# Where the first decay table of a chunked recurrence is kept: PSUM or SBUF

## The chip, the cores and the metric

The kernel runs on one core of a Trainium2 chip. The metric is the device time of one launch in microseconds (us). Engines are named as in the profile: PE is TensorE (matmul), DVE is VectorE, ACT is ScalarE, POOL is GpSimd, and SP issues most of the transfers. The runs lie between 174.58 and 174.9 us.

## The reference

Two parts, one after the other. The first is a linear recurrence over 768 steps, for 4 sequences, 8 heads and head size 48; the second is a two-layer network over the 3072 resulting rows with a smooth gate between.

```python
def _attn_ref(r, k, v, w, u):                 # r, k, v: (4, 8, 768, 48); w, u: (8, 48)
    ...
    for t in range(S):
        kt, vt, rt = (k[:, :, t].copy(), v[:, :, t].copy(), r[:, :, t].copy())
        cur = np.einsum('bhd,bhe->bhde', u[None] * kt, vt)
        y[:, :, t] = np.einsum('bhd,bhde->bhe', rt, state + cur)
        state = w[None, :, :, None] * state + np.einsum('bhd,bhe->bhde', kt, vt)

def _moe_ref(x, w_in, w_out):                 # (3072, 384) x (384, 2048), then x (2048, 384)
    h = x @ w_in
    g = np.where(h >= 1, h, np.where(h <= -1, 0.0, (h + 1) ** 2 / 4))
    return (g @ w_out).astype(np.float32)
```

## The kernel before

**The work and its names.** The 768 steps are cut into 6 chunks of 128 rows, one row per partition. A *group* g is one chunk of two sequences: groups 0 and 1 are the first chunk of sequences 0, 1 and of 2, 3, groups 2 and 3 the second chunk, and so on to 11. A *unit* is one sequence of a group; `Ks.0.1` is step `Ks` of group 0, unit 1, and `T.2` is step `T` of unit number 2, that is group 1, unit 0. Groups 0 and 1 are handled by unit, in tiles of 128x384 (8 heads of 48); later groups as a whole, 128x768.

**The decay.** Inside a chunk, decay is put on the operands: row t of R is multiplied by w^(t-64), row t of K by w^(63-t). The two tables of these powers are made on ACT by `exp(scale * log w)`, with a scale per partition (`dn_col` for K, `up_col` for R) and log w spread over all partitions by a matmul (`bcw`, tile `wb` in PSUM). The kernel makes each of them twice: at the start in PSUM, as the two halves of tile `tab` (steps `Wdn_p`, `Wup_p`, line 264), and a little later in SBUF, as `Wdn` and `Wup` (lines 257, 253). Groups 0 and 1 read `tab`, later groups read `Wdn` and `Wup`.

**The steps of a unit.** `load.K`, `load.R`, `loadV` are transfers from SP's queue. `Ks` and `Rs` (line 334) are the decayed K and R in bf16. `KU` (line 344) is K times u, `RKU` (351) R times that, `usum` (364 on DVE, 362 on ACT) its sum over a head, `V` the cast of V, `V2` (376) V times that sum (the profile shows its tile as `V`). `T` and `TT` turn `Ks` and `Rs` on PE and copy them out of PSUM; `A` (413) is the product of the turned two; `AT` masks it, either on DVE (428) or as a copy on ACT (419) and a select on POOL (423). `Sp` (439) and `Y` (448, 453) are the matmuls with V and with the state, `Tm` (483; 491 in the first chunk) and `decay` (496, POOL) the step of the state, `sbf` its bf16 copy, `y` (475) the output rows, `X` and `xT` their turn. Then `mm1` (533, tile `hp`), `relu` (541), `square` (546), `gate` (551, tile `gt`) and `mm2` (561, tile `op`) are the network.

**What sets the order.** A string `ORDER` lists every step; one token is a step with its numbers, `@D`, `@P` or `@A` for the engine and `:` with buffer numbers. Each engine does its instructions in the order of this list, and waits by semaphores only for what it reads or overwrites. The loads of the weights (`w_in`, `w_out`) stand on POOL's queue, between POOL's products: the first two pieces of `w_in` behind `Rs.2.0`. `~n` on a token puts n small matmuls on zeros ahead of a step on PE.

**Where the tiles lie.** PSUM has two tiles of one bank (`bank0`, `bank1`) and three tiles of two banks (`h0` to `h2`), shared by tag. `tab` lies in `h2` until the last product of group 1 has read it. POOL's instructions here read and write SBUF only.

Of the kernel before, what the change touches and what calls it, by code (L numbers as in the profile page):

```python
# [39 lines left out]
loadV.1.1 RKU.1.1@P AT.0.0 load.R.2.0:1 Ks.1.1@D V.1.1@A T.1:0~2 Tm.1@D usum.0.1@A Y.0:1~16 AT.2.0:0 TT.1@D:0 y.0:1  # L40
T.3:1~7 warm.6.h.2 V2.0.1@D Sp.0:0~4 usum.1.0@A:0 TT.3@A:1 A.1:2 X.0:1~4 Tm.0@D load.K.2.0:1 Sp.3:0 xT.0@A:1
Ks.2.0@D:0 A.3:0 Y.2:1~4 AT.1.1:1 Rs.2.0@P:0 Tm.3@D loadV.2.0:0 w_in.0 w_in.1 V2.1.0@P:0 T.5:1~8 sbf.1@A T.4:2~2
TT.5@A:1 AT.1.0 w_out.0 y.2:1 AT.3.0:2 w_in.2 Y.1:0~4 warm.2.h.0 A.5:1 y.1:2 usum.1.1@D X.1:1~2 Y.3:0~4 AT.5.0:0
TT.4@A:2 V2.1.1@P mm1.0.0.0:2 xT.1@A A.4:0~7 y.3:0 AT.4.0:2 X.2:1~4 load.K.3.0:2 V.2.0@A:1 xT.2@A:0 X.3:0 KU.2.0@P:1
mm1.0.0.1 mm1.0.1.0:0 w_out.2 xT.3@A mm1.0.1.1 RKU.2.0@D:0 usum.2.0@D:1 w_out.1 Sp.5:1 V2.2.0@P:1 mm1.1.1.-1:1
relu.0.0:1 Tm.5@D:1 Y.5:1~2 load.R.3.0:1 square.0.0:1 relu.0.1:0 gate.0.0:0 sbf.0@D square.0.1:0 Y.4:0~2 y.5:1 y.4:2
mm1.1.0.-1:2 gate.0.1:8 relu.1.1:1 X.4:0~2 xT.4@D:2 square.1.1:1 relu.1.0:0 gate.1.1:9 mm2.0.0.0:1 mm1.0.2.-1:0 Sp.4:0
Tm.4@D:0 mm1.0.3.-1:1 square.1.0:0 decay.5 mm2.0.1.0:0 gate.1.0:4 relu.0.2:0 square.0.2:1 Ks.3.0@P:2 KU.3.0@D:1
mm1.1.2.-1:2 gate.0.2:3 mm2.0.0.1 relu.0.3:1 sbf.2@D mm2.0.0.2 square.0.3:0 gate.0.3:0 w_out.3 mm1.1.3.-1:0 Rs.3.0@D:2
load.K.4.0:0 loadV.3.0:0 KRT.K.3:0 mm2.0.0.3 KRT.R.3:1 mm2.0.1.1 relu.1.2:0 square.1.2:1 mm2.0.1.2 relu.1.3:1  # L50
RKU.3.0@P:0 gate.1.2:8 o.0.0@A:1 X.5:1 usum.3.0@D:1 xT.5@A mm2.0.1.3 square.1.3:1 mm1.2.3.-1:2 o.0.1@A mm2.1.0.0:1
sbf.3@A V.3.0@D:1 Sp.6:0 gate.1.3:6 mm2.1.0.1 decay.4 mm2.1.0.2 A.7:1 relu.2.3:0 mm2.1.0.3 A.6:0 load.R.4.0:0
Ks.4.0@P:1 Tm.6@D:0 V2.3.0@P:1 o.1.0@A:0 AT.7.0:3 Sp.7:0 Y.7:1 AT.6.0:1 loadV.5.0:1 mm1.2.0.-1:1 Tm.7@D:1 load.K.5.0:1
decay.6 Y.6:0 mm1.2.2.-1:0 square.2.3:1 y.6:1 relu.2.0:1 y.7 load.R.5.0:2 square.2.0:0 Rs.4.0@P:1 gate.2.3:0
relu.2.2:0 mm2.1.1.0:1 mm2.1.1.1 xT.6:0 KRT.R.4:1 KRT.K.4:0 square.2.2:1 V.5.0@A:4 gate.2.0:9 gate.2.2:3 mm2.1.1.2
mm1.2.1.-1:2 relu.2.1:1 sbf.4@A loadV.4.0:1 square.2.1:1 decay.7 mm2.2.0.0:0 mm2.1.1.3 o.1.1@D KU.5.0@P:0 mm1.3.1.-1:1
relu.3.1:1 gate.2.1:6 mm1.3.2.-1:0 RKU.5.0@P:0 mm2.2.1.0:1 KU.4.0@D:0 mm2.2.0.1 sbf.5@D square.3.1:0 usum.5.0@D:0
gate.3.1:5 Rs.5.0@P:0 RKU.4.0@P:1 mm1.3.0.-1:2 mm2.2.1.1 load.K.6.0:2 relu.3.2:0 mm2.2.0.2 square.3.2:1 out.0
mm2.2.0.3 Ks.5.0@P:2 out.1 A.8:1 gate.3.2:4 A.9:0 mm2.2.1.2 usum.4.0@D:1 V.4.0@A:1 V2.4.0@P:1 relu.3.0:1 KU.6.0@P:1
# [44 lines left out]
def kernel(  # L104
# [157 lines left out]
    def table(what, i, col):  # L262
        t = tiles["tab"][:, i, :DM].rearrange("p (h d) -> p h d", h=H)
        nc.scalar.activation(flat(t), flat(tiles["wb"]), AF.Exp, scale=col, bias=0.0)
# [64 lines left out]
    def scaled(e, bk, g, j, what):  # L329
        j0, j1 = span(g, j)  # L330
        if j == 0:
            tiles[what + "s", g] = padded[what + "s"][bk[0]]
# [1 line left out]
        engines[e].tensor_mul(of_unit(dst, j0, j1)[:, :, :, :D], rep(tab, j1 - j0), of_unit(tiles[what, g], j0, j1))  # L334
# [322 lines left out]
```

## Time and profile before

| | us |
|---|---|
| median of 3 runs | 174.81 (174.58 to 174.9) |
| the profiled execution | 174.86 |
| its span (first to last instruction) | 173.1 |
| busy: PE, DVE, ACT, POOL | 164.1, 137.5, 133.5, 111.3 |

In the profile's rows an instruction is named by engine, line and out<-in, with the number of the tile left out; in brackets stands the idle time of the engine just before it, and what ended that. `PEld` is PE's load of weights. In the chain that ended last, each row is a stretch of work that released the next one; "issue" is time in which the engine waited for nothing that the profile shows. A timeline row that ends in x2 holds two instructions and the time of both. PE's matmuls overlap, so that a row's time is longer than its distance to the next. Rows of the windows view give, for each stretch, its length and for each engine busy time and count, and at the end the granted clock of PE (1.00 throughout), the share of the DMA engines and GB/s.

### The profile page before, as it was taken

What the parts mean: (1) busy time and instruction counts of PE and PEld (TensorE: products, weight loads), DVE (VectorE), ACT (ScalarE), POOL (GpSimd) and SP (SyncE); (2) the same over time, 40 slices, a digit from 0 to 9 for tenths busy, and PEclk for the clock granted to TensorE, in tenths of its full rate; (3) what the DMA queues carried; (4) which work ended last, traced back from release to release, by engine and by line L of the source; (5) the groups of instructions that cost most, each with busy time, mean ns of one, the idle gap of its engine ahead of it and who ended that gap; (6) DMA issues with size and microseconds to landing.
All of it is one profiled execution on the core that took longest, in us unless ns stands there. A gap on an engine that the chain in (4) does not pass through costs nothing.

```text
span 173.1 us, 4227 instructions
## 1 busy us (share of the span) xinstructions
PE 164.1 (95%) x1712; PEld 125.7 (73%) x1712; DVE 137.5 (79%) x175; ACT 133.5 (77%) x193; POOL 111.3 (64%) x92
## 2 busy tenths in 40 slices
...
GB/s 115 210 208 232 204 191 200 182 204 213 205 167 188 202 253 201 125 196 246 153 204 205 202 223 175 229 121 207 162 253 127 139 0 140 0 45 140 0 91 91
...
## 3 DMA queue, kind: packets, MB, share of 16 engines
...
q10 hardware_dynamic: 148, 0.13, 0.2%
q14 instruction: 6, 0.05, 0.1%
...
## 4 chain that ended last, share of the span: by engine, by line
PE 73%; DVE 9%; DMA 6%; SPq 4%; issue 3%; POOL 2%; ACT 1%; ACTq 0%
PE op L561 34%; PE hp L533 31%; DMA w_in_sb<-in_moe_w_in_dram 4%; SPq L311 4%; DVE gt L551 3%; PE A L413 3%; DMA R<-in_r_dram 2%; PE Y L448 2%; PE Y L453 2%; DVE Rs L334 1%; PE Sp L439 1%; POOL Rs L334 1%; DVE Tm L483 1%; DVE AT L428 1%; ACT sq L546 1%
## 5 line engine op out<-in xcount | busy, mean ns | idle before, releaser
L533 PE MATMUL hp<-xT,w_in_sb 128*128 128x256 bf16 (+1 forms) x600 | 70.1, 268 | 0.6 <-DVE AT L428 0.4
L561 PE MATMUL op<-w_out_sb,gt 128*128 128x384 bf16 (+2 forms) x400 | 69.6, 320 | 0.0
L551 DVE SCALAR_TENSOR_TENSOR gt<-sq,hp 128x1024 bf16<-128x1024 f32 x48 | 57.8, 1215 | 8.9 <-ACT sq L546 8.4
L533 PEld LDWEIGHTS <-w_in_sb 128*128 128x128 bf16 x600 | 55.4, 98 | 9.6 <-DVE gt L551 0.7
L541 ACT ACTIVATE pt<-hp 128x1024 f32<-128x1024 f32 x48 | 48.7, 1017 | 10.3 <-PE hp L533 9.7
L546 ACT ACTIVATE sq<-pt 128x1024 f32<-128x1024 f32 x48 | 50.5, 1058 | 2.9 <-DVE gt L551 2.0
L561 PEld LDWEIGHTS <-gt 128*128 128x128 bf16 x400 | 36.8, 98 | 20.4 <-DVE gt L551 0.5
L428 DVE TENSOR_TENSOR AT<-A,umask 128x1024 bf16<-128x1024 f32 x22 | 26.5, 1219 | 4.1 <-PE A L413 4.1
L351 POOL TENSOR_TENSOR RKU<-R,KU 128x768 f32<-128x768 f32 (+1 forms) x13 | 20.4, 1572 | 10.2 <-DMA R<-in_r_dram 6.3
L344 POOL TENSOR_TENSOR KU<-K,u_bc 128x768 f32<-128x768 f32 (+1 forms) x11 | 17.6, 1600 | 5.2 <-DMA K<-in_k_dram 5.2
L496 POOL TENSOR_TENSOR state<-Tm,wCm 128x384 f32<-128x384 f32 x16 | 16.8, 1053 | 1.6 <-DVE Tm L483 0.8
L334 POOL TENSOR_TENSOR Rs<-Wup,R 128x768 bf16<-128x768 f32 x9 | 16.4, 1826 | 2.1 <-DMA R<-in_r_dram 2.1
L334 POOL TENSOR_TENSOR Ks<-Wdn,K 128x768 bf16<-128x768 f32 x9 | 16.4, 1824 | 1.5 <-PE Sp L439 1.5
L376 POOL TENSOR_TENSOR V<-V,diag 128x768 f32<-128x768 bf16 (+1 forms) x11 | 15.3, 1390 | 2.8 <-DVE diag L364 2.4
L212 ACT COPY oo<-op 128x384 f32<-128x384 f32 x18 | 8.5, 473 | 10.7 <-PE op L561 9.2
L475 DVE TENSOR_TENSOR yy<-Y,V 128x384 bf16<-128x384 f32 x18 | 9.7, 553 | 3.8 <-PE Y L453 3.0
L453 PE MATMUL Y<-V,AT 128*128 128x48 bf16 x192 | 11.0, 183 | 0.3 <-POOL AT L423 0.3
L483 DVE TENSOR_TENSOR Tm<-Sp,state 128x384 f32<-128x384 f32 x16 | 8.8, 552 | 2.9 <-PE Sp L439 2.5
L364 DVE TENSOR_REDUCE diag<-RKU 128x16 f32<-128x768 f32 (+1 forms) x12 | 10.5, 879 | 0.0
L453 PEld LDWEIGHTS <-AT 128*128 128x128 bf16 x192 | 9.4, 96 | 1.5 <-issue 0.5
L216 ACT CAST V<-VF 128x768 bf16<-128x768 f32 (+1 forms) x11 | 8.1, 739 | 0.7 <-DMA VF<-in_v_dram 0.7
L448 PE MATMUL Y<-state_bf,RT 128*128 128x96 bf16 x72 | 8.5, 204 | 0.0
...
## 6 DMA issues: line engine op xcount, KB each, us to landing
...
```

Of the source, the lines that this page charges most:

```text
L334: engines[e].tensor_mul(of_unit(dst, j0, j1)[:, :, :, :D], rep(tab, j1 - j0), of_unit(tiles[what, g], j0, j1))
L344: engines[e].tensor_mul(of_unit(tiles["KU", g], j0, j1), of_unit(tiles["K", g], j0, j1), rep(u_bc, j1 - j0))
L351: engines[e].tensor_mul(of_unit(tiles["RKU", g], j0, j1), of_unit(tiles["R", g], j0, j1), of_unit(tiles["KU", g], j0, j1))
L376: engines[e].tensor_mul(tiles["V2", g][:, hs, :], tiles["V", g][:, hs, :], tiles["diag", g][:, hs].unsqueeze(2).to_broadcast([P, hs.stop - ...
L428: nc.vector.tensor_mul(t.rearrange("p i n t -> p (i n) t"), tiles.pop(("A", n)).rearrange("p i n t -> p (i n) t"), umask.unsqueeze(1).to_b ...
L453: nc.tensor.matmul(t[:, 2 * p + i, :], tiles["AT", n][:, i, p, :], tiles["V", g][:, j * H + 2 * p + i, :], start=(c == 0), stop=True, skip ...
L496: nc.gpsimd.tensor_mul(states[(g % BP) * UNITS + j], tiles.pop(("Tm", n)), wCm)
L533: nc.tensor.matmul(hp[:, f, cols], w_in_sb[:, i, n0 : n0 + P], tiles["xT", g][:, units, i, :], start=(i == 0), stop=(i == nK - 1), skip_gr ...
L541: nc.scalar.activation(tiles["pt", g, q], tiles["hp", g, q], AF.Relu, bias=0.5, scale=0.5)
L546: nc.scalar.activation(tiles["sq", g, q], tiles.pop(("pt", g, q)), AF.Square, bias=0.0)
L551: nc.vector.scalar_tensor_tensor(out=gt, in0=tiles.pop(("sq", g, q)), scalar=1.0, in1=tiles.pop(("hp", g, q)), op0=ALU.min, op1=ALU.max)
L561: nc.tensor.matmul(t, tiles["gt", g, q][:, f, j * P : (j + 1) * P], w_out_sb[:, n, cols], start=(n == 0), stop=(n == nF - 1),)
```

## The change

The table for K is no longer made in PSUM first. Step `Wdn_p` goes; step `Wdn`, which writes to SBUF, moves to its place, and the one of later is gone with it. `tab` now holds one table, that for R, in one bank instead of two, and is taken from PSUM by `Wup_p`. `Ks` reads `Wdn` in all groups; `Rs` of groups 0 and 1 still reads `tab`. Besides these, `ORDER` is the same, token for token.

```diff
-... u_bc@A Wdn_p:2 load.K.0.0:2 Wup_p wcol:1 wCm Ks.0.0@D:1 V.1.0@A:0
+... u_bc@A Wdn load.K.0.0:2 Wup_p:2 wcol:1 wCm Ks.0.0@D:1 V.1.0@A:0
...
-loadV.0.0:1 V.0.0@D:2 Wdn loadV.0.1 V.0.1@A usum.0.0@D:1 KU.0.1@P RKU.1.0@P:1 Wup load.R.0.1 Ks.0.1@D RKU.0.1@P
+loadV.0.0:1 V.0.0@D:2 loadV.0.1 V.0.1@A usum.0.0@D:1 KU.0.1@P RKU.1.0@P:1 Wup load.R.0.1 Ks.0.1@D RKU.0.1@P Rs.0.1@D
...
-    def table(what, i, col):
-        t = tiles["tab"][:, i, :DM].rearrange("p (h d) -> p h d", h=H)
-        nc.scalar.activation(flat(t), flat(tiles["wb"]), AF.Exp, scale=col, bias=0.0)
-        tiles["tab", what] = t
-
-    @step
-    def Wdn_p(e, bk):
-        tiles["tab"] = psum(f"h{bk[0]}", [P, 2, 4 * P], F32, "tab")
-        table("K", 0, dn_col)
-
     @step
     def Wup_p(e, bk):
-        table("R", 1, up_col)
+        t = psum(f"h{bk[0]}", [P, 4 * P], F32, "tab")
+        tiles["tab"] = t[:, :DM].rearrange("p (h d) -> p h d", h=H)
+        nc.scalar.activation(flat(tiles["tab"]), flat(tiles["wb"]), AF.Exp, scale=up_col, bias=0.0)
...
-        dst, tab = tiles[what + "s", g], tiles["tab", what] if g < TABLES else {"R": Wup, "K": Wdn}[what]
+        dst, tab = tiles[what + "s", g], tiles["tab"] if what == "R" and g < TABLES else {"R": Wup, "K": Wdn}[what]
```

Two places show it in the engines' own order. On ACT, at the start, with the semaphores waited for in brackets; before:

```order
L212 COPY u_bc<-ub 128x384 [waits PE_49]
L264 ACTIVATE tab<-wb,dn_col 128x384 [waits DVE_49,PE_49]
L264 ACTIVATE tab<-wb,up_col 128x384 [waits Activation_49]
L287 ACTIVATE wc_col<-wc 128x4 [waits PE_49]
L290 COPY wCm<-wc_col 48x4x48 [waits DVE_49,Activation_49]
L290 COPY wCm<-wc_col 48x4x48
L216 CAST V<-VF 128x384 [waits DMAHW4_49]
L212 COPY TT<-T 128x1024 [waits PE_49]
L257 ACTIVATE Wdn<-wb,dn_col 128x384
L216 CAST V<-VF 128x384 [waits DMAHW1_49]
L253 ACTIVATE Wup<-wb,up_col 128x384
```

and after:

```order
L212 COPY u_bc<-ub 128x384 [waits PE_49]
L257 ACTIVATE Wdn<-wb,dn_col 128x384 [waits DVE_49,PE_49]
L266 ACTIVATE tab<-wb,up_col 128x384
L279 ACTIVATE wc_col<-wc 128x4 [waits PE_49]
L282 COPY wCm<-wc_col 48x4x48 [waits DVE_49,Activation_49]
L282 COPY wCm<-wc_col 48x4x48
L216 CAST V<-VF 128x384 [waits DMAHW4_49]
L212 COPY TT<-T 128x1024 [waits PE_49]
L216 CAST V<-VF 128x384 [waits DMAHW1_49]
L253 ACTIVATE Wup<-wb,up_col 128x384
```

One activation is gone from behind `TT`; `Wdn` is made first, and the table for R has no wait on ACT's own table any more. On DVE, the first products of groups 0 and 1; before:

```order
L334 TENSOR_TENSOR Ks<-tab,K 128x8x48 [waits DMAHW5_49,Activation_49]
L334 TENSOR_TENSOR Rs<-tab,R 128x8x48 [waits DMAHW6_49]
L334 TENSOR_TENSOR Ks<-tab,K 128x8x48 [waits DMAHW1_49]
L334 TENSOR_TENSOR Rs<-tab,R 128x8x48 [waits DMAHW3_49]
L219 TENSOR_REDUCE V<-VF 128x384 [waits DMAHW0_49]
L364 TENSOR_REDUCE diag<-RKU 128x8 [waits Pool_49]
L334 TENSOR_TENSOR Ks<-tab,K 128x8x48 [waits DMAHW7_49]
```

and after:

```order
L326 TENSOR_TENSOR Ks<-Wdn,K 128x8x48 [waits DMAHW5_49,Activation_49]
L326 TENSOR_TENSOR Rs<-tab,R 128x8x48 [waits DMAHW6_49,Activation_49]
L326 TENSOR_TENSOR Ks<-Wdn,K 128x8x48 [waits DMAHW1_49]
L326 TENSOR_TENSOR Rs<-tab,R 128x8x48 [waits DMAHW3_49]
L219 TENSOR_REDUCE V<-VF 128x384 [waits DMAHW0_49]
L356 TENSOR_REDUCE diag<-RKU 128x8 [waits Pool_49]
L326 TENSOR_TENSOR Ks<-Wdn,K 128x8x48 [waits DMAHW7_49]
```

Nothing moves on DVE: `Ks` reads another tile, and `Rs.0.0` has a wait of its own on ACT. The order on POOL, SP and PE stays as it was.

More of the change, by code (lines that the diff above doesn't have):

```diff
@@ L35 @@
 ORDER = """
-load.K.1.0:0 load.R.1.0:2 lw bcu:1 bcw:0 loadV.1.0:0 u_bc@A Wdn_p:2 load.K.0.0:2 Wup_p wcol:1 wCm Ks.0.0@D:1 V.1.0@A:0
+load.K.1.0:0 load.R.1.0:2 lw bcu:1 bcw:0 loadV.1.0:0 u_bc@A Wdn load.K.0.0:2 Wup_p:2 wcol:1 wCm Ks.0.0@D:1 V.1.0@A:0
 KU.0.0@P:1 load.R.0.0:0 load.K.0.1 RKU.0.0@P:0 Rs.0.0@D:0 Ks.1.0@D:2 Rs.1.0@D:1 T.0:1 KU.1.0@P:0 TT.0@A:0 Sp.2:1~2
-loadV.0.0:1 V.0.0@D:2 Wdn loadV.0.1 V.0.1@A usum.0.0@D:1 KU.0.1@P RKU.1.0@P:1 Wup load.R.0.1 Ks.0.1@D RKU.0.1@P
-Rs.0.1@D T.2:1~2 load.K.1.1 A.0:0 load.R.1.1 TT.2@D:1 AT.0.1:3 Sp.1:0 Tm.2@D A.2:1~2 V2.0.0@D:1 KU.1.1@D Rs.1.1@D
@@ L40 @@
[L40 to L59, printed above, removed]
```

29 lines of the change are left out of this document (25 added, 4 removed).

## The prediction

> **What bounds the kernel now.** The page's first part comes first: it says which engine is filled over the whole span.
>
> ```profile
> PE 164.1 (95%) x1712; PEld 125.7 (73%) x1712; DVE 137.5 (79%) x175; ACT 133.5 (77%) x193; POOL 111.3 (64%) x92
> ```
>
> TensorE is busy for 95%, so a delay costs time only if it makes TensorE start later, or opens a gap in it. Next is the chain that ended last, between 6 and 50 us, to see what TensorE waits for at the start. Columns: start, us, what.
>
> ```profile
> 7.25 3.91 DMA R<-in_r_dram
> ...
> 17.66 6.09 DMA w_in_sb<-in_moe_w_in_dram
> 23.79 0.84 PE hp L533 x12
> ...
> 40.24 1.95 DVE Rs L334
> ...
> 42.45 1.22 DVE gt L551
> ...
> 43.72 1.48 PE hp L533 x12
> 45.20 0.65 PE op L561 x4
> ```
>
> The second layer's first matmul at 23.79 waits for `w_in`, whose issue stands on POOL's queue at 17.66, behind POOL's work for the first groups. That work is reached through a transfer: `R` for step `Rs.0.1`, issued at 7.25, landed at 11.16. After 43.72 this chain is nearly all TensorE. So what counts is the moment at which POOL issues `w_in`, and what becomes of a shift there before 43.72. The timeline of the window that the change touches (start, us, engine, line, out<-in):
>
> ```profile
> 6.48 0.56 ACT L264 ACTIVATE tab<-wb,dn_col 128x384 f32<-128x384 f32 x1 [0.80 <-PE wb L244]
> 6.64 0.99 POOL L344 TENSOR_TENSOR KU<-K,u_bc 128x384 f32<-128x384 f32 x1 [2.80 <-DMA K<-in_k_dram]
> 7.07 0.56 ACT L264 ACTIVATE tab<-wb,up_col 128x384 f32<-128x384 f32 x1
> 7.66 0.56 DVE L334 TENSOR_TENSOR Ks<-tab,K 128x384 bf16<-128x384 f32 x1 [4.11 <-ACT tab L264]
> 7.72 1.00 POOL L351 TENSOR_TENSOR RKU<-R,KU 128x384 f32<-128x384 f32 x1
> 8.13 0.55 DVE L334 TENSOR_TENSOR Rs<-tab,R 128x384 bf16<-128x384 f32 x1
> 8.60 0.55 DVE L334 TENSOR_TENSOR Ks<-tab,K 128x384 bf16<-128x384 f32 x1
> 8.67 1.95 POOL L344 TENSOR_TENSOR KU<-K,u_bc 128x384 f32<-128x384 f32 x2
> ...
> 9.38 1.01 ACT L212 COPY TT<-T 128x1024 bf16<-128x1024 bf16 x1
> ...
> 10.29 0.59 ACT L257 ACTIVATE Wdn<-wb,dn_col 128x384 f32<-128x384 f32 x1
> ...
> 10.53 0.55 DVE L334 TENSOR_TENSOR Ks<-tab,K 128x384 bf16<-128x384 f32 x1
> 10.58 1.95 POOL L351 TENSOR_TENSOR RKU<-R,KU 128x384 f32<-128x384 f32 x2
> ...
> 11.18 0.56 DVE L334 TENSOR_TENSOR Rs<-tab,R 128x384 bf16<-128x384 f32 x1
> ...
> 12.78 0.55 DVE L376 TENSOR_TENSOR V<-V,diag 128x384 f32<-128x384 bf16 x1
> ...
> 13.25 0.55 DVE L344 TENSOR_TENSOR KU<-K,u_bc 128x384 f32<-128x384 f32 x1
> 13.88 1.00 POOL L351 TENSOR_TENSOR RKU<-R,KU 128x384 f32<-128x384 f32 x1 [1.34 <-DVE KU L344]
> ...
> 14.18 0.55 DVE L334 TENSOR_TENSOR Ks<-tab,K 128x384 bf16<-128x384 f32 x1
> ...
> 14.83 1.09 POOL L423 TENSOR_SCALAR_AFFINE_SELECT AT<-AT 128x1024 bf16<-128x1024 bf16 x1
> 15.89 1.83 POOL L334 TENSOR_TENSOR Rs<-Wup,R 128x768 bf16<-128x768 f32 x1
> ...
> 17.31 0.82 DVE L376 TENSOR_TENSOR V<-V,diag 128x384 f32<-128x384 bf16 x1
> ```
>
> POOL is filled without a gap from 6.64 to 12.53, then has 1.34 us free, then runs through to the issue. DVE's four `Ks<-tab` take 0.55 us beside a busy POOL. That is the row that the change puts at risk: their first input moves from PSUM to SBUF, so both inputs are then in SBUF. What such an instruction does beside POOL is shown later in this trace, from the timeline, from the page, and from the groups by form:
>
> ```profile
> 39.89 1.82 POOL L351 TENSOR_TENSOR RKU<-R,KU 128x768 f32<-128x768 f32 x1 [6.29 <-DMA R<-in_r_dram]
> 40.16 2.37 DVE L334 TENSOR_TENSOR Rs<-Wup,R 128x768 bf16<-128x768 f32 x1
> 41.68 1.70 POOL L496 TENSOR_TENSOR state<-Tm,wCm 128x384 f32<-128x384 f32 x1
> ...
> L496 POOL TENSOR_TENSOR state<-Tm,wCm 128x384 f32<-128x384 f32 x16 | 16.8, 1053 | 1.6 <-DVE Tm L483 0.8 <-ACT pt L541 0.6
> ...
> L344 DVE TENSOR_TENSOR KU<-K,u_bc 128x768 f32<-128x768 f32 x2 | 1.9, 952 | 0.0
> ```
>
> Of DVE's products of that size with both inputs in SBUF, `KU` takes 0.95 us; `Rs<-Wup,R` at 40.16 takes 2.37. It ends at 42.53, 0.82 after POOL's `RKU` (41.71). POOL's `state` at 41.68 takes 1.70 where the other fifteen average (16 x 1.053 - 1.70)/15 = 1.01, and ends at 43.38, 0.85 after DVE's 42.53. The two take turns: the blocked DVE instruction ends its own time less 0.13 after POOL's, the blocked POOL instruction its own time less 0.16 after DVE's. The smaller size agrees: `V2.0.1` at 17.31 ends at 18.13, 0.41 after POOL's `Rs` (17.72); its twin at 12.78, beside an idle POOL, takes 0.55.
>
> The Trainium skill, "SBUF — State Buffer", section "Who interferes with whom", says that a DVE instruction with two SBUF inputs contends with a GpSimd instruction that reads SBUF, and that whichever issues second fully blocks until the first is done. The trace agrees on who blocks (2.37 us against 0.95) and differs a little on the price, since about 0.15 us of the second one overlaps the end of the first. Taken to the letter (0.55 after POOL, 1.00 after DVE) it gives the fourth rival's sum.
>
> **The change, part by part.**
>
> Removed: one activation on ACT, `Wdn`, 0.59 us at 10.29. ACT's next path item before it, the copy `TT` at 9.38 to 10.39, stands ahead of it and doesn't move; the next one that others wait for, the copy of `AT`, waits for TensorE's `A`, itself behind `TT`. Worth nothing. No queue loses or gains a transfer, and DVE, POOL, SP and TensorE keep their order.
>
> Changed: the first table is written to SBUF: 0.59 instead of 0.56 by the `Wdn` row, so done at 7.07 instead of 7.04. `Ks.0.0` used to start at 7.66, 0.03 after the second table (7.07 + 0.56 = 7.63), so it waited for both; now it needs the first alone and can start at 7.10. The second table needn't wait for the first any more and is done by 7.63 at the latest. A gain of 0.56 at the head of DVE's queue is on offer, but POOL holds `KU.0.0` until 7.63.
>
> Collisions, worked out with the turns above. DVE starts one instruction 0.47 after the last (7.66, 8.13, 8.60); a blocked `Ks` ends 0.41 after POOL's; a blocked POOL product of 1.00 ends 0.85 after DVE's.
> 1. `Ks.0.0`, ready at 7.10, blocked by `KU.0.0` to 7.63, ends at 8.04. `RKU.0.0` ends at 8.89 (before: 8.72). `Rs.0.0`, which still reads PSUM, starts at 7.96.
> 2. `Ks.1.0`, ready at 8.43, ends at 8.89 + 0.41 = 9.30. `KU.1.0` ends at 10.15 (before: some 9.65, half of the pair).
> 3. `Rs.1.0` starts at 9.22; three starts later `Ks.0.1` is ready at 10.63. `KU.0.1` runs to 11.13, so `Ks.0.1` ends at 11.54 (before 11.08), `RKU.1.0` at 12.39 (before 11.55).
> 4. `Rs.0.1` starts at 11.46 (before 11.18: here the transfer ended the wait, so nothing gained ahead of it would have counted). `V2.0.0` is ready at some 13.0 instead of 12.78 and now meets `RKU.0.1`, which runs 12.39 to 13.36 instead of ending at 12.53: it ends at 13.77 (before 13.33). POOL's free 1.34 us is spent: +0.44 on `KU.1.1` and on POOL's `RKU.1.1`, 14.32 to 15.32.
> 5. `Ks.1.1` is ready at 14.62, blocked to 15.32, ends at 15.73 (before 14.73: +1.00). POOL's `AT` select behind it ends 1.09 - 0.16 later, at 16.66 (before 15.92: +0.74).
>
> POOL then does `Rs.2.0` and issues `w_in` at about 18.40, +0.74. DVE's own +1.00 goes back to the same +0.74 when `V2.0.1` waits for `Rs.2.0` as it does now. Behind that, up to 23.79, DVE, POOL and ACT run in each other's wake, so I take +0.74 for TensorE's start too. Bounds for it: 0 if none of the collisions happens; +0.31 if only the last does (`RKU.1.1` to 14.88, `Ks.1.1` to 15.29, select to 16.22); +0.74 with all.
>
> What of it reaches the end. Two more views: DMA by windows, and TensorE and SP around the gap.
>
> ```profile
> 16.00:18.00 2.00, 1.98 (x37) 1.84 (x37) 2.00 (x4) 2.00 (x19) 2.00 (x2) 1.00 1.28 223
> ...
> 36.00:40.00 4.00, 4.00 (x33) 2.90 (x32) 4.00 (x5) 3.94 (x5) 0.11 (x1) 1.00 1.27 205
> ...
> 27.52 0.37 SPq L311 DMA_DIRECT2D R<-in_r_dram  x1
> ...
> 42.78 0.81 PE L561 MATMUL op<-w_out_sb,gt 128*128 128x384 bf16 x4
> ```
>
> DMA (last two numbers: share and GB/s) is full at 17 us, before `w_in` is asked for, and still at 40. `R` for group 3 is issued at 27.52 and lands at 39.89, 12.4 us later. A `w_in` issue that is 0.74 late leaves the engines to the loads already waiting, so the bytes ahead of that `R` are done at about the same time: I take its landing as unmoved (bounds 0 and +0.74). Then `RKU.3.0` and the `Rs.3.0` that it blocks end at 41.71 and 42.53 as before, though DVE comes to `Rs.3.0` 0.74 later, and the `gt` that TensorE needs ends at 43.67 as before. TensorE, pushed by 0.74, finishes the `op` group of 42.78 not at 43.43 (42.78 and 0.65, the time of four such matmuls in the chain's row at 45.20) but at 44.17; the gap before 43.72, some 0.28, is eaten. Shift at the end: 0.74 - 0.28 = +0.46. If the landing moves along, +0.74.
>
> **Sum.** The profiled execution took 174.86 us (span 173.1 and 1.76 around it), 0.05 above the median of 174.81. 174.86 + 0.46 = 175.32; against the median 175.27. I forecast 175.3, +0.3%.
>
> **Rivals.**
> - No collision costs anything: a table read again and again is not the second stream of `Rs<-Wup,R`, or DVE slips in between POOL's reads. For it: the blocked rows are few. Against: `Rs<-Wup,R` has the very shape of the new `Ks<-Wdn,K`. Then `Ks.0.0` is 0.56 early, `R` at 11.16 eats that, and the change does nothing measurable: 174.8.
> - Collisions, but mostly swallowed: POOL's free 1.34 us holds the first three and only the last passes, +0.31, less the gap of 0.28: 174.85 to 175.1. For it: the fourth step turns on `RKU.0.1` outlasting DVE's 13.00, by 0.36 us only.
> - All of it passes, since `R` for group 3 is issued behind DVE's later `RKU.2.0` and lands later by as much: 174.81 + 0.74 = 175.55.
> - Full turns without overlap: the same five steps with 0.55 and 1.00 give +1.50 on `KU.1.1`, +2.1 at the select, +1.8 at the end: 176.6. Against it: three rows above with 0.13 to 0.16 of overlap. It is what the Trainium skill says in the section of “SBUF — State Buffer” named above, taken to the letter.
> - Faster: `R` for `Rs.0.1` lands before 10.6 and POOL lets DVE in. Then DVE's 0.56 passes to `KU.1.1`, the `w_in` issue and, if group 3's `R` comes along, the end: 174.3. It decides only if the landing at 11.16 moves by more than half a microsecond, with no collision; the 2.80 us that POOL waits for its first `K` says that the loads set the pace here.
>
> **Chances.** Forecast 0.34; all passes 0.17; full turns 0.04: slower 0.55. Swallowed 0.18, no collision 0.17: same 0.35. Faster 0.10. "Same" means within 0.2%, 0.35 us, about what this kernel's runs can tell from no change (they lie 0.32 apart). The forecast alone spans 175.1 to 175.5. The range leaves out the faster case and the full turns, and holds the rest: 174.6 to 175.8.
>
> **What the profile after would show.** DVE's `Ks<-Wdn,K` of 128x384 at 0.55 (no collision) or about 0.9 to 1.1 (four collisions: 0.94, 0.87, 0.92, 1.11); POOL's `RKU` and `KU` of that size at 1.0 or about 1.2; no `ACT tab` wait beyond the first table; `w_in` issued at 17.7 or 18.4; the gap before the group at 43.72 gone or not. I am wrong if `Ks` takes 0.55 beside a busy POOL, if `w_in` is issued by 17.9, or if it is issued at 18.4 and the end doesn't move: then there is more slack behind it than the one gap.

## The result, and the profile after

| | median, us | range, us | runs |
|---|---|---|---|
| before, in the same series | 174.90 | 174.58 to 175.58 | 6 |
| after | 176.07 | 175.91 to 176.74 | 6 |

The changed kernel is slower: the ratio is 1.0068, 95% interval [1.0045, 1.0091], that is +1.2 us. The forecast was 175.3 with a range of 174.6 to 175.8: the sign came out as forecast, the size is two and a half times the +0.46 that was worked out, and the time lies outside the range. The profiled execution took 176.18 us (span 174.4, granted clock 1.00), 1.3 more than the one of before. One kernel below, `last_only`, was profiled in an execution at a granted clock of 0.77 (span 212.7 us), so only its times are used and the table of runs leaves it out.

First the page: engines over the span, and the group of the network's second matmul with the idle time ahead of it.

```profile
PE 164.4 (94%) x1712; PEld 125.5 (72%) x1712; DVE 137.7 (79%) x175; ACT 133.3 (76%) x192; POOL 112.4 (64%) x92
...
L553 PE MATMUL op<-w_out_sb,gt 128*128 128x384 bf16 (+2 forms) x400 | 69.6, 320 | 0.6 <-DMA w_out_sb<-in_moe_w_out_dram 0.6
```

TensorE does the same work (164.4 against 164.1), and the span around it is longer: gaps, not work. One gap has a name at once, a wait of 0.6 for a piece of `w_out`, which the second layer reads. Now the start, in the timeline of after, against the forecast of the collisions:

```profile
6.82 0.99 POOL L336 TENSOR_TENSOR KU<-K,u_bc 128x384 f32<-128x384 f32 x1 [2.98 <-DMA K<-in_k_dram]
...
7.15 1.08 DVE L326 TENSOR_TENSOR Ks<-Wdn,K 128x384 bf16<-128x384 f32 x1 [3.60 <-ACT Wdn L257]
...
7.90 1.19 POOL L343 TENSOR_TENSOR RKU<-R,KU 128x384 f32<-128x384 f32 x1
...
8.62 0.88 DVE L326 TENSOR_TENSOR Ks<-Wdn,K 128x384 bf16<-128x384 f32 x1
9.05 2.27 POOL L336 TENSOR_TENSOR KU<-K,u_bc 128x384 f32<-128x384 f32 x2
...
10.81 0.92 DVE L326 TENSOR_TENSOR Ks<-Wdn,K 128x384 bf16<-128x384 f32 x1
...
11.28 2.27 POOL L343 TENSOR_TENSOR RKU<-R,KU 128x384 f32<-128x384 f32 x2
...
13.19 0.77 DVE L368 TENSOR_TENSOR V<-V,diag 128x384 f32<-128x384 bf16 x1
...
14.51 1.00 POOL L343 TENSOR_TENSOR RKU<-R,KU 128x384 f32<-128x384 f32 x1 [0.96 <-DVE KU L336]
...
14.82 1.10 DVE L326 TENSOR_TENSOR Ks<-Wdn,K 128x384 bf16<-128x384 f32 x1
...
15.46 1.41 POOL L415 TENSOR_SCALAR_AFFINE_SELECT AT<-AT 128x1024 bf16<-128x1024 bf16 x1
...
18.60 1.70 POOL L289 DMA_DIRECT2D w_in_sb<-in_moe_w_in_dram  x2
```

All four `Ks` collide (1.08, 0.88, 0.92 and 1.10 us instead of 0.55), `V2.0.0` does too (0.77), POOL's products grow as forecast, and `w_in` is issued at 18.60: 0.94 later than before, of which 0.18 was there from the start, since the first `K` landed that much later in this execution (POOL's `KU` at 6.82, before 6.64).

TensorE and POOL behind that, in the timeline of before (the rows at 39.89 and 43.72 stand in the prediction) and then of after:

```profile
20.49 1.08 POOL L423 TENSOR_SCALAR_AFFINE_SELECT AT<-AT 128x1024 bf16<-128x1024 bf16 x1
21.53 0.80 POOL L301 DMA_DIRECT2D w_out_sb<-in_moe_w_out_dram  x1
...
25.80 1.55 POOL L301 DMA_DIRECT2D w_out_sb<-in_moe_w_out_dram  x2
```

```profile
24.49 0.83 PE L525 MATMUL hp<-xT,w_in_sb 128*128 128x128 bf16 x12
...
31.67 1.47 PE L525 MATMUL hp<-xT,w_in_sb 128*128 128x256 bf16 x12
...
39.40 1.46 PE L553 MATMUL op<-w_out_sb,gt 128*128 128x384 bf16 x8 [0.58 <-DMA w_out_sb<-in_moe_w_out_dram]
...
42.59 2.54 POOL L343 TENSOR_TENSOR RKU<-R,KU 128x768 f32<-128x768 f32 x1 [8.30 <-DMA R<-in_r_dram]
...
44.95 1.49 PE L525 MATMUL hp<-xT,w_in_sb 128*128 128x256 bf16 x12
```

TensorE starts the network at 24.49 instead of 23.79 (+0.70). The group at 44.95 is the one that stood at 43.72 (+1.23), and from there the two run alike. The new waits lie between: 0.58 at 39.40 for `w_out`, while the `R` of group 3 releases POOL only at 42.59 (before 39.89). The chain that ended last, in after, tells where that wait comes from:

```profile
16.39 1.14 DVE AT L420
...
17.57 0.55 PE T L204 x7
...
20.64 0.92 ACT AT L411
...
21.63 1.09 POOL AT L415
22.72 0.75 POOL w_out_sb L293
...
26.90 0.75 POOL w_out_sb L293
27.65 11.71 DMA w_out_sb<-in_moe_w_out_dram
...
39.40 1.46 PE op L553 x8
```

This chain doesn't go through the late `w_in` issue. It goes from DVE's `AT` through TensorE's turn (`T`) and ACT's copy of another unit's `AT` to POOL's select, and then to the `w_out` issues behind that select. The select starts at 21.63 instead of 20.49, so the pieces of `w_out` are asked for 1.1 us later. The last of them lands 11.7 us after its issue.

Last, DMA by windows (share and GB/s at the end), before and then after:

```profile
22.00:26.00 4.00, 3.63 (x67) 3.11 (x68) 3.36 (x6) 2.31 (x5) 3.82 (x5) 1.00 1.23 190
26.00:30.00 4.00, 4.00 (x68) 3.75 (x66) 3.97 (x5) 3.94 (x6) 2.72 (x3) 1.00 1.15 202
```

```profile
22.00:26.00 4.00, 3.93 (x81) 3.41 (x78) 3.77 (x6) 3.14 (x4) 3.92 (x5) 1.00 1.09 171
26.00:30.00 4.00, 4.00 (x63) 3.78 (x62) 3.88 (x5) 3.40 (x5) 3.08 (x4) 1.00 1.11 160
```

The share stays above 1 (the engines are filled), but fewer bytes move: 190 and 202 GB/s before, 171 and 160 after.

### The profile page after: what moved, and what is told of

The parts are those of the page before. It is cut to its first block, busy times and chain, and to the rows that moved or that the text cites. A ratio compares the mean times of both kernels' runs of the same rounds, so it can differ in the third digit from the quotient of the medians.

```text
span 174.4 us, 4227 instructions
## 1 busy us (share of the span) xinstructions
PE 164.4 (94%) x1712; PEld 125.5 (72%) x1712; DVE 137.7 (79%) x175; ACT 133.3 (76%) x192; POOL 112.4 (64%) x92
## 3 DMA queue, kind: packets, MB, share of 16 engines
q0 software_dynamic: 3312, 3.15, 11.8%
HBM read 20.45 MB, written 4.72 MB: 144 GB/s over the span
## 4 chain that ended last, share of the span: by engine, by line
PE 76%; DVE 7%; DMA 7%; POOL 3%; ACT 2%; issue 2%; DVEq 0%; ACTq 0%; POOLq 0%
PE op L553 35%; PE hp L525 29%; DMA w_out_sb<-in_moe_w_out_dram 7%; PE A L405 3%; PE Y L445 2%; PE Y L440 2%; PE Sp L431 1%; DVE AT L420 1%; DVE Ks L326 1%; POOL KU L336 1%; PE ub L249 1%; DVE Rs L326 1%; POOL w_out_sb L293 1%; PE wb L244 1%; POOL AT L415 1%
## 5 line engine op out<-in xcount | busy, mean ns | idle before, releaser
L533 ACT ACTIVATE pt<-hp 128x1024 f32<-128x1024 f32 x48 | 48.7, 1018 | 10.7 <-PE hp L525 10.1
L343 POOL TENSOR_TENSOR RKU<-R,KU 128x768 f32<-128x768 f32 (+1 forms) x13 | 21.5, 1660 | 10.9 <-DMA R<-in_r_dram 8.3
L212 ACT COPY oo<-op 128x384 f32<-128x384 f32 x18 | 8.5, 473 | 10.7 <-PE op L553 9.1
L488 POOL TENSOR_TENSOR state<-Tm,wCm 128x384 f32<-128x384 f32 x16 | 16.0, 1004 | 1.0 <-ACT pt L533 0.6
```

Source lines behind the costliest of these rows:

```text
L343: engines[e].tensor_mul(of_unit(tiles["RKU", g], j0, j1), of_unit(tiles["R", g], j0, j1), of_unit(tiles["KU", g], j0, j1))
L488: nc.gpsimd.tensor_mul(states[(g % BP) * UNITS + j], tiles.pop(("Tm", n)), wCm)
L533: nc.scalar.activation(tiles["pt", g, q], tiles["hp", g, q], AF.Relu, bias=0.5, scale=0.5)
```

## The experiments

All ratios are to the kernel before in the same series; 95% intervals in brackets.

### Repeats, and the late piece of `w_out`

The kernels before and after once more, unaltered:

> The kernel before once more, for a second profile and as the measure of noise. Ratio 1.000 within 0.002. Theory A: no wait of TensorE for w_out, group 3's R lands at 39.9 +- 0.4 us. Theory B: the landing times of w_out and R move by a microsecond or more between two profiles of the same kernel.

> The changed kernel once more, unaltered, timed in more rounds and with a second profile. Theory A (the late weight loads): TensorE's start is 0.7 us late from the collisions, and the second w_out piece, issued 1.05 us late behind them, adds a wait of about 0.6 us at 38 to 39 us; both are in every execution, so the second profile shows the wait again (0.4 to 0.8 us) and the time is 1.1 to 1.3 us above before. Theory B (chance in the transfers): the wait for w_out was this one profile's; it is missing here and the time is 0.7 to 0.9 us above before.

Before: 174.98 us, 0.9993 [0.9970, 1.0017]. After: 176.47, 1.0087 [1.0056, 1.0119]. The loss is real, and the executions of after spread from 175.32 to 176.93. The wait of 0.58 at 39.40 isn't in all of them: the second profile of after, of its quickest execution (span 173.6), has only one of 0.18, at 41.40, though `w_out` is issued at 22.37 there.

Then the order of the two pieces is exchanged, in after and in before, so that the piece that TensorE waited for at 39.40 is issued first:

```diff
-mm1.0.1.0:0 w_out.2 xT.3@A mm1.0.1.1 RKU.2.0@D:0 usum.2.0@D:1 w_out.1 Sp.5:1 ...
+mm1.0.1.0:0 w_out.1 xT.3@A mm1.0.1.1 RKU.2.0@D:0 usum.2.0@D:1 w_out.2 Sp.5:1 ...
```

> The changed kernel with the two w_out pieces that stand next to each other on POOL's queue in the other order, so that the piece which the second layer reads first (w_out.1) is asked for first. Theory A: the wait of 0.58 us goes (w_out.1 then lands near 36.7 us, before TensorE asks at 38.7), and w_out.2, which is read 0.65 us later, lands at about 39.3: at most 0.1 us of wait is left; the time falls by 0.4 to 0.6 us, to about 0.6 us above before. Theory C (the wait only hides another one, R of group 3 and the gate behind Rs.3.0, landing 2.5 us late): the wait goes but the gap at 44 us grows by as much, and the time falls by less than 0.15 us.

> The kernel before with the same swap of w_out.1 and w_out.2. There the piece lands at 37.2 us, 0.7 us before TensorE wants it. Theory A: nothing changes, 174.9 within 0.25 us. If it becomes faster by over 0.3 us, the pieces were a limit before the change too, in executions other than the profiled one.

In after: 175.98, 1.0059 [1.0035, 1.0083], against 1.0087 for after in the same series, so that the two intervals overlap; in before 174.98, 0.9999 [0.9978, 1.0020]. TensorE's timeline of the exchanged after:

```profile
42.14 2.11 PE L553 MATMUL op<-w_out_sb,gt 128*128 128x384 bf16 x12 [0.63 <-DMA w_out_sb<-in_moe_w_out_dram]
...
44.99 1.48 PE L525 MATMUL hp<-xT,w_in_sb 128*128 128x256 bf16 x12
```

The wait at 39.40 is gone, and one of 0.63 stands at 42.14; the group behind it begins at 44.99, as in after. The wait belongs to whatever was landing late, not to the one piece. So the next step takes the need for the pieces away: the second layer of group 0 reads the first piece for all four, and leaves out the other three.

```diff
-                t, tiles["gt", g, q][:, f, j * P : (j + 1) * P], w_out_sb[:, n, cols],
+                t, tiles["gt", g, q][:, f, j * P : (j + 1) * P], w_out_sb[:, n % FG if g == 0 else n, cols],
```

> The changed kernel, where the second layer of group 0 reads the first piece of w_out for all four pieces (so group 0's rows are computed with wrong weights), with every transfer as it was: TensorE needn't wait for the later pieces at 38 to 42 us. Theory A (start shift 0.5, the rest is the wait for w_out): 175.3 to 175.5, the waits for w_out gone and the group near 44 us at +0.4 to +0.55 against before. Theory C (behind the wait for w_out stands group 3's R with Rs.3.0 and the gate, equally late): the wait goes, the group near 44 us stays at +1.0 or more, and the time stays above 175.8.

> The kernel before with the same change of weights in group 0. Theory A: in most executions w_out is in time, so the median stays at 174.9 within 0.15 us; executions above 175.3, which were a quarter of the runs, become rarer if a late w_out made them.

In after: 175.94, 1.0057 [1.0032, 1.0083]; in before 174.95, 0.9990 [0.9966, 1.0015]. No wait for `w_out` is left, and most of the loss is. Two rows of this after's timeline:

```profile
41.99 2.52 POOL L343 TENSOR_TENSOR RKU<-R,KU 128x768 f32<-128x768 f32 x1 [7.71 <-DMA R<-in_r_dram]
...
46.50 0.33 PE L431 MATMUL Sp<-V,Ks 128*128 128x96 bf16 x4 [0.22 <-DVE V L219]
```

`R` of group 3 still lands at 41.99, its product ends at 44.51, DVE's work behind it is late, and TensorE waits for that. What is late is a whole batch of transfers, and behind a wait for one of them stands the wait for the next.

### Which collision carries the loss

The collisions are undone in part. In before, only the last `Ks` of group 1 reads the SBUF table (`last_only`); in after, that one alone reads a table in PSUM, made where `Wdn` stood before (`first_three`):

```diff
 last_only
-... tiles["tab", what] if g < TABLES else {"R": Wup, "K": Wdn}[what]
+... tiles["tab", what] if g < TABLES and (what, g, j) != ("K", 1, 1) else {"R": Wup, "K": Wdn}[what]
 first_three
-... tiles["tab"] if what == "R" and g < TABLES else {"R": Wup, "K": Wdn}[what]
+... tiles["tab", what] if g < TABLES and (what == "R" or (g, j) == (1, 1)) else {"R": Wup, "K": Wdn}[what]
```

> The kernel before, with one of the four K products (Ks.1.1, the last) reading the table in SBUF, which is there by 10.9 us. Theory A (turns between DVE and POOL, then the late weight loads): Ks.1.1 takes 1.1 us instead of 0.55, POOL's select behind it 1.4 instead of 1.09, w_in is issued 0.3 us later; TensorE's first-layer group at 31 us is 0.2 to 0.3 us late, and the time rises by 0.1 to 0.5 us. Rival D (one collision is swallowed by POOL's other waits): w_in issued within 0.1 us of before, the time within 0.2 us.

> The changed kernel, with the last of the four K products reading a table in PSUM, which ACT makes later, where Wdn stood before. Three collisions are left. Theory A: Ks 0.85 to 1.1, 0.88 and 0.92 us, V2.0.0 0.78 us, POOL's RKU.1.1 0.45 to 0.6 us later than before, Ks.1.1 at 0.55; w_in 0.45 to 0.6 us late, the time 0.4 to 0.9 us above before. Rival E (only the last collision counts, since POOL's free 1.34 us holds the first three): w_in within 0.1 us of before and the time within 0.2 us.

The last collision alone: 175.23, 1.0007 [0.9984, 1.0029]. The first three alone: 175.19, 1.0003 [0.9975, 1.0031]. Either part costs nothing that can be measured (0.3% is the upper end of either interval), and both together cost 0.7%. In the timeline of `first_three`, the last `Ks`, the `w_out` issue behind the select, and `R` of group 3:

```profile
14.56 0.54 DVE L334 TENSOR_TENSOR Ks<-tab,K 128x384 bf16<-128x384 f32 x1
...
21.84 0.80 POOL L301 DMA_DIRECT2D w_out_sb<-in_moe_w_out_dram  x1
...
40.50 2.53 POOL L351 TENSOR_TENSOR RKU<-R,KU 128x768 f32<-128x768 f32 x1 [6.99 <-DMA R<-in_r_dram]
```

The first three collisions put DVE 0.38 behind before (`Ks.1.1` at 14.56, before 14.18) and the `w_out` issue 0.31 behind (21.84, before 21.53), and the kernel absorbs that.

A third kernel undoes the last collision in another way, by order: `Ks.1.1` is put ahead of `KU.1.1` on DVE, so that it runs while POOL waits.

```diff
-... V2.0.0@D:1 KU.1.1@D Rs.1.1@D loadV.1.1
-RKU.1.1@P AT.0.0 load.R.2.0:1 Ks.1.1@D V.1.1@A ...
+... V2.0.0@D:1 Ks.1.1@D KU.1.1@D Rs.1.1@D loadV.1.1
+RKU.1.1@P AT.0.0 load.R.2.0:1 V.1.1@A ...
```

> The changed kernel with Ks.1.1 ahead of KU.1.1 on DVE, where POOL is idle waiting for KU.1.1, so that the last collision goes and KU.1.1 comes 0.47 us later. Theory H: the select ends some 0.15 us later than in the changed kernel, but DVE is done 0.5 us earlier; 0.1 to 0.5 us of the loss comes back: 175.5 to 176.0. If the last collision were what tips it over (three alone cost nothing): 175.0 to 175.3.

175.29 against 174.99, 1.0042 [1.0014, 1.0070]: the median gives most of the loss back and the ratio about half of it, with an interval that overlaps that of after. POOL's last `RKU` starts later by the `Ks` put ahead of it, and single executions still reach 177.4. No version beat before.

### Is it the port, and whose reading

POOL's `KU` and `RKU` of groups 0 and 1 are replaced by three memsets each, some 1.3 us in place of 1.0, which write SBUF and read nothing (the term with u is thereby left out in these groups):

```diff
+        if e == "P" and g < TABLES:
+            for _ in range(3):
+                nc.gpsimd.memset(of_unit(tiles["RKU", g], j0, j1), 0.0)
+            return
```

> The changed kernel, where POOL's products KU and RKU of groups 0 and 1 are replaced by three memsets each into the same tile (so those groups' bonus term is left out of the output): POOL is as busy, but only writes SBUF. If the turns are about reading, the four Ks take 0.55 us beside a busy POOL, and V2.0.0 too; POOL's memsets keep 0.41 us. If any access of POOL to SBUF collides with a DVE product of two SBUF inputs, Ks takes 0.7 us or more where a memset runs, or memsets stretch to 0.6 us or more.

One execution, 175.01. Its timeline:

```profile
6.41 2.68 POOL L338 MEMSET KU<- 128x384 f32 x6
7.15 0.56 DVE L326 TENSOR_TENSOR Ks<-Wdn,K 128x384 bf16<-128x384 f32 x1 [3.60 <-ACT Wdn L257]
...
13.34 1.42 POOL L423 TENSOR_SCALAR_AFFINE_SELECT AT<-AT 128x1024 bf16<-128x1024 bf16 x1 [0.31 <-ACT AT L419]
...
14.19 0.98 DVE L326 TENSOR_TENSOR Ks<-Wdn,K 128x384 bf16<-128x384 f32 x1
```

`Ks<-Wdn` beside six memsets takes 0.56, and the next two, also beside memsets, 0.55 each. Beside the select, which reads SBUF, the last one takes 0.98, and the select 1.42 instead of 1.09. So in these rows two SBUF inputs on DVE cost time only against a POOL instruction that reads SBUF. The Trainium skill, "SBUF — State Buffer", section "Who interferes with whom", limits the contention of a DVE instruction with two SBUF inputs to a GpSimd instruction that reads SBUF; these rows agree.

### POOL's delay, or DVE's

Before is delayed by hand. First POOL alone: a memset of 128x768 ahead of the first `w_in` issue (`before_late`), and the same memset further ahead, in front of the select of `AT.0` (`before_sel`).

```diff
+    late = const.tile([P, 768], F32, name="late")
...
+            nc.gpsimd.memset(late, 0.0)
```

> The kernel before with nothing but a memset of 128x768 on POOL ahead of the first w_in (some 0.8 us; its tile is read by nothing). No K product collides. Theory F (a late POOL queue is the whole cause): w_in is issued at about 18.5 us and lands at about 24 us all the same; all weight loads behind it are 0.6 to 1.0 us late, group 3's R lands at 41.5 us or later, and the time rises by 0.5 to 1.1 us as in the changed kernel. Theory G (DVE's own delay by the collisions is needed): the time rises by less than 0.3 us.

> The kernel before with the same memset of 128x768 on POOL (0.74 us), now ahead of the select of AT.0 instead of behind Rs.2.0, so that Rs.2.0 and V2.0.1 on DVE, which waits for it, are late too; no K product collides. Theory H (delays alone; the engines' chain and the weight loads both count): the first-layer group at 31.0 us comes 0.3 to 0.5 us late and the time rises by 0.4 to 0.9 us. Theory J (only the collisions of the changed kernel do it): below 0.25 us, as with the memset behind Rs.2.0.

`before_late`: 175.13, 1.0007 [0.9990, 1.0025]. `before_sel`: 175.17, 1.0020 [1.0000, 1.0040]. The second one's timeline:

```profile
15.62 1.09 POOL L427 TENSOR_SCALAR_AFFINE_SELECT AT<-AT 128x1024 bf16<-128x1024 bf16 x1
...
18.44 1.71 POOL L297 DMA_DIRECT2D w_in_sb<-in_moe_w_in_dram  x2
...
22.10 0.81 POOL L301 DMA_DIRECT2D w_out_sb<-in_moe_w_out_dram  x1
```

This is the very shift that the prediction put on POOL, with `w_in` issued at 18.44 (forecast 18.40), and it costs 0.2% (at most 0.4%), about the 0.3% that was forecast and not the 0.7% that was measured. Then DVE alone: the last `Ks` of group 1 is done three times, from PSUM, with nothing added on POOL (`before_dve`); and both delays together (`before_both`).

```diff
-        engines[e].tensor_mul(of_unit(dst, j0, j1)[:, :, :, :D], rep(tab, j1 - j0), of_unit(tiles[what, g], j0, j1))
+        for _ in range(3 if (what, g, j) == ("K", 1, 1) else 1):
+            engines[e].tensor_mul(of_unit(dst, j0, j1)[:, :, :, :D], rep(tab, j1 - j0), of_unit(tiles[what, g], j0, j1))
```

> The kernel before with the last K product of group 1 done three times on DVE, from PSUM (0.93 us more on DVE, nothing on POOL). Theory H: DVE's 0.9 us is mostly swallowed, since V2.0.1 waits for POOL's Rs.2.0 anyway (0.3 us of it) and TensorE's start waits for w_in: 0.0 to 0.4 us. If DVE's delay were the whole cause: 0.9 to 1.2 us.

> Both delays in the kernel before: 0.74 us on POOL ahead of the select, 0.93 us on DVE at the last K product, which are the two that the changed kernel shows, and no collision. Theory H: the changed kernel's time is reproduced, 0.8 to 1.3 us above before, with the group at 31 us 0.4 to 0.7 us late and the stretch from there to 46 us 0.3 us or more longer. Theory J: below 0.5 us.

`before_dve`: 176.56, 1.0106 [1.0063, 1.0148]. `before_both`: 176.40, 1.0084 [1.0052, 1.0116]. DVE's delay alone gives the whole loss, and POOL's adds nothing to it that can be measured. The timeline of `before_dve`:

```profile
14.26 1.73 DVE L335 TENSOR_TENSOR Ks<-tab,K 128x384 bf16<-128x384 f32 x3
...
17.72 1.71 POOL L297 DMA_DIRECT2D w_in_sb<-in_moe_w_in_dram  x2
...
21.69 1.09 POOL L424 TENSOR_SCALAR_AFFINE_SELECT AT<-AT 128x1024 bf16<-128x1024 bf16 x1 [1.41 <-ACT AT L420]
22.73 0.81 POOL L301 DMA_DIRECT2D w_out_sb<-in_moe_w_out_dram  x1
...
24.50 0.83 PE L534 MATMUL hp<-xT,w_in_sb 128*128 128x128 bf16 x12
...
35.07 1.48 PE L534 MATMUL hp<-xT,w_in_sb 128*128 128x256 bf16 x12 [0.99 <-DMA w_in_sb<-in_moe_w_in_dram]
...
40.45 1.46 PE L562 MATMUL op<-w_out_sb,gt 128*128 128x384 bf16 x8 [0.46 <-DMA w_out_sb<-in_moe_w_out_dram]
...
43.47 2.56 POOL L352 TENSOR_TENSOR RKU<-R,KU 128x768 f32<-128x768 f32 x1 [9.17 <-DMA R<-in_r_dram]
```

`w_in` is issued at 17.72, as in before. Then POOL stands still for 1.41 us until ACT has copied `AT`, which hangs on DVE through TensorE, and the `w_out` issue is at 22.73, as in after (22.67). This shows one path of the delay: DVE, TensorE, ACT, the select on POOL, and the weight issues queued behind that select. There is a second one. TensorE starts the network at 24.50, as late as in after (24.49), though `w_in` was asked for in time and landed at 17.72 + 5.9 = 23.6. DVE's `RKU.2.0` follows that start, and SP issues the `R` of group 3 when `RKU.2.0` has ended: at 28.21, in after at 28.20, in before at 27.52. TensorE then waits for a late `w_in` piece (0.99) and a late `w_out` piece (0.46), and `R` comes at 43.47. No run here delays the select or TensorE's start by that much and leaves the other in place, so what each path contributes isn't shown.

### An earlier issue of `w_in`

The two first issues of `w_in` are moved ahead of POOL's product `Rs.2.0`, in after and in before:

```diff
-... AT.1.1:1 Rs.2.0@P:0 Tm.3@D loadV.2.0:0 w_in.0 w_in.1 V2.1.0@P:0 ...
+... AT.1.1:1 w_in.0 w_in.1 Rs.2.0@P:0 Tm.3@D loadV.2.0:0  V2.1.0@P:0 ...
```

> The changed kernel with the first two pieces of w_in moved ahead of Rs.2.0 on POOL's queue, so that they are issued at about 16.9 us instead of 18.6 and Rs.2.0 runs behind them. Theory F: w_in lands by 22.5 us, TensorE's first layer starts by engines alone, group 3's R lands at 41 us or earlier, and most of the loss is gone: 175.0 to 175.5. Theory G: DVE's delay stays, and 175.8 to 176.3 with it; so it would be too if the later Rs.2.0 (1.7 us) held up TensorE's turn of group 2, which the wait of that step will show.

> The kernel before with the same move. Theory F: w_in lands 1 us or more before 23.8, where TensorE waits for it now, so the start is set by the engines (23.3 to 23.6 us), and the time is 174.4 to 174.9. Rival: the later Rs.2.0 meets V2.0.1 and Ks.2.0 on DVE, which read SBUF twice, and costs more than the earlier loads bring: 175.0 to 175.8.

After: 176.30, 1.0076 [1.0056, 1.0097]; before: 175.65, 1.0049 [1.0023, 1.0075]. An earlier issue helps neither and harms before. A row of DVE's timeline in that before:

```profile
17.09 2.53 DVE L376 TENSOR_TENSOR V<-V,diag 128x384 f32<-128x384 bf16 x1
```

`Rs.2.0` now runs later, just as DVE comes to `V2.0.1`, which reads SBUF twice and takes 2.53 us instead of 0.82. Its row even begins 0.29 ahead of that of `Rs.2.0` (17.38), and yet it is DVE that waits; why isn't shown. In after it takes 2.30. There no transfer is late any more (`R` of group 3 is there by 39.21), but TensorE begins the group of 31.67 at 32.62: the same loss by another way. The step that was to be helped made a new collision.

### The runs side by side

Read from each kernel's profile, in us: when DVE begins the `AT` that the chain above starts from, when POOL issues the first `w_out`, how long the next two pieces take to land (median of the two), when `R` of group 3 releases POOL, and when the group of eight `op` begins that stands at 45.86 in before. Sorted by the issue of `w_out`. The two kernels with the earlier `w_in`, which have another order on POOL, are left out.

| kernel | DVE `AT` | `w_out` issued | landing | `R` of group 3 | `op` x8 | span |
|---|---|---|---|---|---|---|
| before_swap | 14.99 | 21.39 | 10.7 | 41.24 | 45.99 | 173.2 |
| before_piece0 | 14.94 | 21.47 | 9.9 | 40.56 | 45.52 | 172.7 |
| before | 15.11 | 21.53 | 9.7 | 39.89 | 45.86 | 173.1 |
| again_before | 15.32 | 21.83 | 9.5 | 39.63 | 45.92 | 173.1 |
| first_three | 15.49 | 21.84 | 9.4 | 40.50 | 45.70 | 172.9 |
| pool_writes | 15.55 | 21.91 | 9.8 | 39.41 | 46.12 | 173.3 |
| before_late | 15.08 | 22.01 | 9.7 | 41.37 | 46.43 | 173.7 |
| before_sel | 15.22 | 22.10 | 10.0 | 41.28 | 46.22 | 173.5 |
| again_after | 16.01 | 22.37 | 9.7 | 41.74 | 46.43 | 173.6 |
| after_piece0 | 16.02 | 22.37 | 10.6 | 41.99 | 46.67 | 173.9 |
| after_swap | 16.23 | 22.58 | 10.9 | 42.62 | 47.31 | 174.5 |
| after | 16.31 | 22.67 | 10.7 | 42.59 | 47.28 | 174.4 |
| before_dve | 16.37 | 22.73 | 11.8 | 43.47 | 48.19 | 175.4 |
| before_both | 16.37 | 22.73 | 11.5 | 43.02 | 47.72 | 174.9 |
| after_reorder | 15.57 | 22.83 | 12.1 | 43.83 | 48.52 | 175.7 |

These are single executions; that of `again_after` is its quickest (175.32) and that of `after_reorder` its slowest (177.4). The span less the column `op` x8 is 127.12 to 127.28 in all of them: all that is lost is lost by 48 us. With the issue at 22.10 or earlier the group of `op` stands within 0.6 of before; with the issue at 22.58 to 22.83, 1.0 to 1.3 later than in before, it is 1.4 to 2.7 late. So the delay grows on the way. `after_reorder` doesn't fit the first column: its `AT` is only 0.46 later than in before and its issue the latest of all, with ACT's copy at 20.70. There POOL's own delay takes part: TensorE waits for the select of `AT.0` until 16.89 (before 15.98). In these last five kernels the two pieces take 10.7 to 12.1 us to land, in the others 9.4 to 10.0 (two exceptions, 10.6 and 10.7), and DMA moves 156 to 178 GB/s between 22 and 30 us, in the others 184 to 211.

The table also shows where a late `R` begins to cost. In all seven kernels where `R` comes at 41.74 or later, the group of `op` begins 4.68 to 4.72 after it; in the other eight the distance is 4.75 to 6.71. Between the two lie POOL's `RKU`, DVE's `usum` and its cast of `V`, and TensorE's `Sp`. In these seven `RKU` takes 2.5 us instead of the 1.82 of before: when `R` comes that late, DVE is already waiting for it too, its `Rs` starts first (in after at 42.46, 0.13 ahead), and now POOL waits for DVE. In after, TensorE's own work behind the late `w_out` piece reaches that group at about the same time; in `after_piece0`, where no piece is waited for, the distance is 4.68 all the same. So in before, with 5.97, the `R` of group 3 has some 1.3 us to spare (an estimate, 5.97 less 4.7), and in these profiles what it is late beyond that passes to the end. `before_swap` agrees: `R` comes 1.35 later than in before, and its `op` group 0.13 later.

One caution on single profiles: in `before_piece0`, `first_three` and `before_swap` this `R` was issued within 0.15 us of before (27.44, 27.43 and 27.67 against 27.52), and it came at 40.56, 40.50 and 41.24, so 0.6 to 1.35 of its lateness can come with the issue in place.

## Why the prediction was right in sign and wrong in size

**The collisions: right.** Forecast for the four `Ks` 0.94, 0.87, 0.92, 1.11, measured 1.08, 0.88, 0.92, 1.10 (the first began beside a `KU` that was itself 0.18 late). With that 0.18 added, the starts and ends of the other steps came out to 0.05 us: POOL's `RKU.1.1` at 14.51 (forecast 14.32), the select's end at 16.87 (16.66). The rivals of no collision and of full turns are out, and with the end at +1.2 so are the swallowed and the faster one.

**The issue of `w_in`: right in time, wrong in weight.** It moved as forecast, but it was not what TensorE waits for. The next row is from the DMA view of after, for the first issue at 18.60 (number, size, us from issue to landing):

```profile
w_in_sb<-in_moe_w_in_dram POOLq DMA_DIRECT2D x1, 384.0 KB, 5.2
```

By the chain in the prediction the first piece had landed at 17.66 + 6.09 = 23.75; in after it landed at 18.60 + 5.2 = 23.8. The later issue landed at the same moment, as in `before_sel` too (18.44 and 5.1). TensorE's +0.70 at 24.49 looks like the +0.74 that was forecast, but it came by another way, and that the two sizes agree is luck: `before_dve`, with `w_in` issued in time, starts the network at 24.50, and POOL's delay alone, in `before_sel`, at 24.14 only, and moved the end by 0.2%.

**The step that failed first: "DVE's own +1.00 goes back to the same +0.74 when `V2.0.1` waits for `Rs.2.0` as it does now."** `V2.0.1` itself did as forecast: it ended 0.95 later (19.08 against 18.13), as POOL's `Rs.2.0` did (0.94, both with the 0.18 from the late `K`). But DVE's delay had left DVE before that. `AT` on DVE stands ahead of `V2.0.1`, and it was 1.20 late (16.31), 1.02 without the 0.18. From `AT` a second path leads through TensorE and ACT to POOL's select and to TensorE's own start. The rows of before:

```profile
15.11 1.22 DVE L428 TENSOR_TENSOR AT<-A,umask 128x1024 bf16<-128x1024 f32 x1
...
19.34 1.02 ACT L419 CAST AT<-A 128x1024 bf16<-128x1024 f32 x1
```

To the select this path had at most 0.13 us to spare: in before the select began at 20.49, as soon as POOL was free, and ACT's copy had ended at 20.36 (19.34 and 1.02). So the select came 1.14 late, 0.96 without the 0.18, and not 0.74, and with it every weight issue behind it. The prediction followed POOL's delay through the queue of POOL and dropped DVE's, the larger one; `before_dve` shows that DVE's alone is enough for the whole loss.

**The step that failed second: "I take its landing as unmoved", with the gap of 0.28 eaten.** It was argued from the `w_in` issue, for which it held. It didn't hold for the `R` of group 3: issued 0.68 later (28.20 in SP's timeline of after, 27.52 before), it released POOL at 42.59 instead of 39.89, +2.7, where the bounds were 0 and +0.74. The term "-0.28" between 31 and 46 us measured +0.74: from the group at 31.67 to the `op` group at 47.28 it took 15.61, in before 14.87 (30.99 to 45.86). With +0.68 at 31.67 that is +1.42 at the group and +1.3 at the end of the span. With `R` in time the gap is eaten about as forecast: in `pool_writes` and `after_early`, where the group at 31 is late as well (31.47 and 32.62) and `R` is there by 39.41 and 39.21, the stretch takes 14.65 and 14.62, that is -0.22 and -0.25. So the term failed by the landing that it rests on. The rival "all of it passes" had the place right, a late `R` of group 3, but let it move by as much as its issue: 175.55.

**What stays open.** Why the landing moves by more than the issue. The lower rate is seen in the five profiles with the latest issue, its cause isn't, and it isn't needed: in `again_after` and `after_piece0` `R` is 1.9 and 2.1 later than in before at 190 to 200 GB/s. Nor is it shown whether the later weight issues or the later issue of `R` itself matter more. That DVE's +0.38 in `first_three` costs nothing while +1.26 in `before_dve` costs 1% goes with where `R` comes, at 40.50 and at 43.47, within the 1.3 us to spare and beyond them; but no run moves that landing alone, and for `last_only` no row shows it.
